# Loads, turns and layer steps at other distances in a fused attention and two-layer kernel

## The chip, the cores and the metric

The kernel runs on one core of a Trainium2 chip. The metric is the time of one execution on the device in microseconds (us); lower is better. A core has TensorE (PE, with its weight loads shown as PEld), VectorE (DVE), ScalarE (ACT), GpSimd (POOL) and SyncE (SP), each with its own queue of instructions that it works through in program order. DMAs are issued from the queues of SP and ACT.

## The reference

Inputs are q, k and v of shape 8 x 8 x 576 x 64 (batch, heads, rows, width), a threshold tau of 0.02, and the weights w_in (512 x 2048) and w_out (2048 x 512), all in 32 bits.

```python
scale = 1.0 / np.sqrt(q.shape[-1])
scores = scale * np.matmul(q, k.transpose(0, 1, 3, 2))
thresh = np.max(scores, axis=-1, keepdims=True) - tau
scores = np.where(scores >= thresh, scores, -1000000000.0)
scores = scores - np.max(scores, axis=-1, keepdims=True)
attn = np.exp(scores)
attn = attn / (np.sum(attn, axis=-1, keepdims=True) + 1e-09)
attn_out = np.matmul(attn, v)
x = attn_out.transpose(0, 2, 1, 3).reshape(B * S, H * D)   # 4608 x 512
h = x @ w_in
g = h - np.tanh(h)
out = g @ w_out
```

## The kernel before

**Pairs and tiles.** Two heads of one batch entry make a pair; there are 32 pairs, four to a batch entry. The 2 x 576 rows of q of a pair make nine tiles of 128 rows, 288 tiles in all. Eight of the nine lie in one head; the ninth holds the last 64 rows of both, and it is the last of an even pair and the first of an odd one. Even tiles are of kind A and odd ones of kind B; most work after the scores is done for an A and its B together.

**What is done to a pair.** q and k are loaded into `raw` tiles (L143 to L204). POOL scales them and splits each into two 16-bit halves, high and low (`split`, L222, three instructions). The split tile is turned so that the width lies on the partitions (`turn`, L297). Pairs 0 to 7 are turned on PE, nine transposes into a tile of PSUM from the pool `ps_big`, which DVE copies to SBUF (L313); pairs from `DUAL` = 8 on are turned by one transposing DMA each for k and q on SP's queue (L301). `swap` (L318) has POOL copy the turned k with its two halves exchanged (kS). `split_v` (L255) has POOL cast v into one of four tiles `vb`. The pools of `raw`, `hl` (split) and `qk` (kT, kS and qT) have two buffers for each name.

**What is done to a tile.** PE computes its scores from kT, kS and qT (L396, or L387 for the shared ninth tiles); DVE scales them into `sc` and keeps their maximum (L406) and makes the bias `nb` (L418); ACT makes `z` with a steep Prelu (L433), which leaves what lies within tau of the maximum and sends the rest far down; z is turned, on PE for pairs 0 to 5 and by a transposing DMA on SP (L440) from pair 6 on; ACT takes the exponential (L461 or L469) into `pT`; PE multiplies by v into `psO` (`attend`, L474); DVE divides (`norm`, L517); PE turns the result (`emit_x`, L537, `psX`) and DVE copies it into `xT`.

**The layers.** One stage m takes 512 rows of one batch entry (the last stage, the 64 remaining rows of all eight). An "h" step is a chunk of 128 of the 2048 hidden columns: four matmuls into `psH` (L565), tanh on ACT into `th` (L578), the subtraction on DVE into `g` (L584). A "y" step is a quarter of the second product for 128 rows: four matmuls into `psY` (L591), and after the fourth quarter a copy `yo` (L603) and a store. `psH` and `psX` share two buffers of PSUM; `psY` has one.

**Order.** The program is unrolled by hand into steps s from -8 to about 291 (the loop at L820). A step issues the scores of tile s + 8, z of tile s + 5, the tanh of h steps of the step before, the exponential of tile s, the layer step of this step if there is one, the subtraction of the h step before, and attend of tile s - 2. At its end it issues what `plan` has for this step: loads, splits, turns, swaps. A last part issues the loads and casts of the weights (POOL casts them at 16 listed steps, `cast_when`). For pair p the plan counts back from step 9p - 8, at which the pair's first tile gets its scores: an entry `("k0", 17)` of `LATER` loads k 17 steps earlier, "q0", "q1", "v0", "v1" are parts of loads, "ks", "qs", "vs" splits, "kt", "qt" turns, "kw" the swap. `LATER` holds for pairs from 8 on, one list for even and one for odd ones; `PREP` and `k_lead` hold for pairs 1 to 7. Loads of pairs from 8 on are issued from ACT's queue (L172), those before from SP's.

The layer steps of stage m = 0 to 6 run beside the attention of the next batch entry, from step 36 (m + 1) + 4 on. `PATTERN` (L622) gives for each of 36 steps whether it holds an h step, a y step or none. The first y steps of a stage are those left over from the stage before. The end, stages 7 and 8, is layers alone.

Of the kernel before, what the change touches and what calls it, by code (L numbers as in the profile page):

```python
# [9 lines left out]
F32 = mybir.dt.float32  # L10
# [8 lines left out]
def kernel(  # L19
# [11 lines left out]
    nc = tc.nc  # L31
    P = 128

    B, H, S, D = q.shape
# [11 lines left out]
    HPAIR = H // 2  # L46
# [5 lines left out]
    TPP = 9  # L52
# [10 lines left out]
    AHEAD = 8  # L63
# [25 lines left out]
    for i in range(NV):  # L89
        vb = const.tile([P, 2, 6, D + 1], BF16, name=f"vb{i}")  # L90
# [8 lines left out]
    for i in range(6):  # L99
# [8 lines left out]
    pool = lambda name, bufs, **kw: ctx.enter_context(  # L108
        tc.tile_pool(name=name, bufs=bufs, **kw)
    )  # L110
    PSUM = bass.MemoryType.PSUM
    raw_pool = pool("raw", 2)
    hl_pool = pool("hl", 2)
    qk_pool = pool("qk", 2)
    sc_pool = pool("sc", AHEAD - MASK + 2)
    st_pool = pool("st", 12)
    z_pool = pool("z", 4)
# [16 lines left out]
    raws = {}  # L134
    DUAL = 8
    AT_ONCE = 1
# [4 lines left out]
    boths = {}  # L141

    def load_part(p, t, part):  # L143


        b, h0 = p // HPAIR, 2 * (p % HPAIR)
        if part == 0:
            both = raw_pool.tile([P, 2, 10, D], F32, name=f"{t}raw", tag=t)
            both = boths[t] = both[:, 0:AT_ONCE, :, :]
            for a in range(AT_ONCE):  # L150
                raws[p + a, t] = both[:, a, :, :]
        both = boths[t]
        rows = {"k": k, "q": q, "v": v}[t][b, h0 : h0 + 2 * AT_ONCE, :, :]
        heads = both.rearrange("p a (h c) d -> p (a h) (c d)", h=2)
        if t == "k":
            dst = both[:, :, 0:TPP, :].rearrange("p a c d -> p a (c d)")
            rows = rows.rearrange("(a h) s d -> a (h s) d", h=2).rearrange(
                "a (p c) d -> p a (c d)", c=TPP
            )
        elif t == "v":  # L160
            rows = rows.rearrange("h (p c) d -> p h (c d)", c=TPP)
            if part == 0:
                dst, rows = heads[0:64, :, 0 : 4 * D], rows[:, :, 0 : 4 * D]
            else:
                dst, rows = heads[64:P, :, :], rows[:, :, 4 * D :]
        elif part == 0:
            dst = heads[:, :, 0 : 4 * D]
            rows = rows[:, 0:512, :].rearrange("h (p c) d -> p h (c d)", c=4)
        else:
            dst = both[:, part - 1, 4, :]  # L170
            rows = rows[2 * part - 2 : 2 * part, 512:S, :].rearrange("h s d -> s h d")
        LOADER.dma_start(out=dst, in_=rows)  # L172

    def load(p, t):
        b, h0 = p // HPAIR, 2 * (p % HPAIR)
        hs = slice(h0, h0 + 2)
        src = {"k": k, "q": q, "v": v}[t]
        eng = nc.sync
        r = raw_pool.tile([P, 2, 10, D], F32, name=f"{t}raw", tag=t)[:, 0, :, :]
        raws[p, t] = r  # L180
        eng.dma_start(
            out=r.rearrange("p (h c) d -> p h (c d)", h=2)[:, :, 0 : 4 * D],
            in_=src[b, hs, 0:512, :].rearrange("h (p c) d -> p h (c d)", c=4),
        )
        rem = src[b, hs, 512:S, :].rearrange("h s d -> s h d")
        if t == "v":
            eng.dma_start(out=r[0:64, 4:10:5, :], in_=rem)
        else:
            eng.dma_start(out=r[:, 4, :], in_=rem)

    def load_first(t, h, eng):

        src = {"k": k, "q": q}[t]
        if (0, t) not in raws:
            raws[0, t] = raw_pool.tile([P, 2, 10, D], F32, name=f"{t}raw", tag=t)[:, 0, :, :]
        r = raws[0, t]
        if h is None:
            rem = src[0, 0:2, 512:S, :].rearrange("h s d -> s h d")
            eng.dma_start(out=r[:, 4, :], in_=rem)
        else:  # L200
            eng.dma_start(
                out=r[:, 5 * h : 5 * h + 4, :].rearrange("p c d -> p (c d)"),
                in_=src[0, h, 0:512, :].rearrange("(p c) d -> p (c d)", c=4),
            )  # L204
# [49 lines left out]

    def split_v(p):  # L255
        r, vb = raws.pop((p, "v")), vbs[p % NV]
        lo = 64 if p >= DUAL else 0
        nc.gpsimd.tensor_copy(
            out=vb[:, :, 0:4, 0:D],
            in_=r.rearrange("p (h c) d -> p h c d", h=2)[:, :, 0:4, :],  # L260
        )
        nc.gpsimd.tensor_copy(out=vb[0:64, :, 4, 0:D], in_=r[lo : lo + 64, 4:10:5, :])
        nc.gpsimd.tensor_copy(out=vb[64:P, :, 5, 0:D], in_=r[lo : lo + 64, 4:10:5, :])

# [12 lines left out]
    def turn_chunk(out, c, lhsT, mixed=True):  # L277
# [4 lines left out]
            out=out, lhsT=lhsT, rhs=rhs, is_transpose=True, start=True, stop=True  # L282
        )

    def k_lead(p):
        if p < HPAIR + 2:
            return 6 if p in (2, 4) or p == HPAIR + 1 else 5 - (p == 1)
        return (6, 6)[1 - p % 2]

    def q_by_dma(p):  # L290

        return p >= DUAL

    def k_by_dma(p):
        return p >= DUAL

    def turn(p, t):  # L297
        hl = hls.pop((p, t))
# [290 lines left out]
    def project(m, ms, part, ps, last, cols=slice(0, d_model)):  # L589
# [31 lines left out]

    PATTERN = lambda m: {  # L622
        0: '-h--h-hh--h-hh-h-hh-h--hh-h--hh-y-yy',
        B - 2: 'hyhyhyhyhyhyhyhyhyhyhyhyhyhyhyhy',
    }.get(m, 'h-yhyhhyhyyhyyhh-yhhyhhy-yhyyh-yyhhy')

    FIRST = 3
    quarters = lambda m: [(m, ms, part) for ms in range(4) for part in range(4)]
# [90 lines left out]
    def w_load(piece):  # L719
# [6 lines left out]
        else:  # L726
# [18 lines left out]

    LATER = {
        0: (
            ("k0", 17), ("q0", 15), ("v0", 13), ("kt", 7), ("q1", 15),
            ("ks", 8), ("v1", 12), ("vs", 6), ("qs", 10), ("qt", 7),
            ("kw", 3),  # L750
        ),
        1: (
            ("k0", 19), ("v1", 14), ("q0", 18), ("v0", 16), ("qs", 11),
            ("q1", 17), ("qt", 8), ("ks", 13), ("vs", 6), ("kt", 10),
            ("kw", 7),
        ),
    }
    for p in range(DUAL, NPAIR):
        first = TPP * p - AHEAD
        at = lambda d, f: plan.setdefault(first - d, []).append(f)  # L760
        for what, d in LATER[p % 2]:
            t, w = what
            f = {
                "0": lambda p=p, t=t: load_part(p, t, 0),
                "1": lambda p=p, t=t: load_part(p, t, 1),
                "2": lambda p=p, t=t: load_part(p, t, 2),
                "s": lambda p=p, t=t: split_v(p) if t == "v" else split(p, t),
                "t": lambda p=p, t=t: turn(p, t),
                "w": lambda p=p, t=t: swap(p) if k_by_dma(p) else None,
            }[w]  # L770
            at(d, f)
    for p in range(1, DUAL):
        first = TPP * p - AHEAD
        for d, f in PREP[3 if p == 1 else 0 :]:
            d -= p == 1 and d == 3
            if p > HPAIR and d >= LDK - 2:
                d = ((16, 14, 12), (17, 15, 13))[1 - p % 2][LDK - d]
            elif d in (7, 8) and q_by_dma(p):
                d = ((9, 9) if d == 7 else (10, 10))[1 - p % 2]
            elif d == 4:  # L780
                d = 4
            elif d == 5:
                d = k_lead(p)
            elif p in (2, 4):
                d = {8: 9, 7: 8}.get(d, d)
            plan.setdefault(first - d, []).append(lambda p=p, f=f: f(p))
        d = (6, 7)[1 - p % 2] if q_by_dma(p) else 3 - (p == 1 or p >= 5)
        d = 4 if p in (2, 4) else d
        plan.setdefault(first - d, []).append(lambda p=p: turn(p, "q"))

    load(0, "v")
# [8 lines left out]
        load(1, t)  # L800
    pieces = w_pieces()
    load_when = [3, 8, 13, 18, 21, 25, 29, 34, 38, 42, 46, 49, 52, 55, 58, 61]
    cast_when = [11, 19, 27] + [4 * i + 32 for i in range(3)] + [3 * i + 44 for i in range(10)]

    todo, stage = [], 0
    fold = const.tile([P, 64], BF16, name="fold")
# [3 lines left out]
            plan.setdefault(-AHEAD, []).extend(plan.pop(at))  # L810


    kinks, wts, atts = {}, {}, {}
    for i in range(NTILE + 3):
        at = i - 4 if i < HPAIR * TPP else i
        atts.setdefault(at + LAG, []).append(i)
        if i < NTILE:
            wts.setdefault(at, []).append(i)
            kinks.setdefault(i // 2 * 2 + 2 - AHEAD if i < 4 else i - MASK, []).append(i)
    for s in range(-AHEAD, NTILE + LAG + 3):  # L820
        p, j = divmod(max(s, 0), TPP)
# [10 lines left out]
        n = s + AHEAD  # L832
# [14 lines left out]
        if s == 0:  # L847
            nc.vector.tensor_tensor(
                out=fold, in0=ident_bf[:, 0:64], in1=ident_bf[:, 64:P], op=ALU.add
# [15 lines left out]
                emit_x(pp - 1)  # L865
        for step in plan.pop(s, []):
            step()
        if s + AHEAD in cast_when:
            w_cast()
        if s + AHEAD in load_when:  # L870
            w_load(next(pieces))

    for _, step in todo:
# [16 lines left out]
    _ = bass_utils  # L890
# [35 lines left out]
```

## Time and profile before

| | us |
|---|---|
| median of 3 runs | 514.31 (512.71 to 514.61) |
| the profiled execution | 509.47 |
| its span, first to last instruction | 507.7 |

| engine | busy us | share of the span |
|---|---|---|
| PE | 484.1 | 95% |
| ACT | 432.7 | 85% |
| DVE | 400.0 | 79% |
| POOL | 291.1 | 57% |

The profile shows one execution, so its parts add up to 507.7 us and not to the median. A line of a group reads: line of the code, engine, operation, output<-inputs, shapes, count, then busy time and mean of one in ns, then the idle time of the engine ahead of it and what ended it. Overlapping matmuls are shown with their latency, so a busy PE may still be pausing; the distance from one start to the next tells more. A wait for several semaphores is put down to the one that came last.

### The profile page before, as it was taken

Reading aid. Unit: us, or ns where it says so; the run is one execution under the profiler, and the core shown is the slowest. Engines: PE = TensorE matmul, PEld = TensorE weight load, DVE = VectorE, ACT = ScalarE, POOL = GpSimd, SP = SyncE. Lnnn points to the kernel's source line nnn. Section 1 sums busy time; section 2 is a strip of 40 time slices with the busy share of each in tenths; the row PEclk is TensorE's granted clock in tenths of the full one; section 3 lists DMA queues with packets and bytes.
Section 4 is the critical chain, followed back from the end, with each engine's and each line's share of the span. In section 5 each row is a group of like instructions: output and inputs, shape, how many; then the busy total and the mean of one; then the engine's idle time right before and its main releaser. Section 6 shows DMA issues by size and latency. Waiting matters only on the chain.

```text
span 507.7 us, 12146 instructions
## 1 busy us (share of the span) xinstructions
PE 484.1 (95%) x4274; PEld 270.4 (53%) x4336; DVE 400.0 (79%) x1149; ACT 432.7 (85%) x617; POOL 291.1 (57%) x390
## 2 busy tenths in 40 slices
PE   8999899888999999999999999999998999999997
PEld 4667566444555555555555555555554555544444
DVE  5899979976989898988898889889887887544440
ACT  5999999988999999999999999999998999533430
POOL 7999999967676657574757575575567500000000
PEclk9999999998999999999999999999999999999999
DMA  6852658999999999999999999999999976211013
GB/s 198 264 163 90 196 176 220 226 189 220 211 245 228 242 227 223 242 249 211 228 228 268 216 228 228 223 231 231 212 220 252 197 131 113 76 41 43 24 40 83
DMA packets 234525, 95.61 MB, mean 188 GB/s; under 512 B 205152, under 2 KB 223840, under 8 KB 234464
## 3 DMA queue, kind: packets, MB, share of 16 engines
q1 hardware_dynamic: 213520, 73.17, 74.7%
q10 hardware_dynamic: 20944, 21.67, 15.7%
q8 instruction: 34, 0.56, 0.5%
q14 instruction: 27, 0.22, 0.1%
HBM read 36.70 MB, written 9.44 MB: 91 GB/s over the span
## 4 chain that ended last, share of the span: by engine, by line
PE 61%; POOL 12%; DMA 10%; ACT 6%; issue 5%; DVE 3%; ACTq 1%; SPq 0%; POOLq 0%
PE psY L591 20%; PE psH L565 16%; PE psS L396 14%; PE psO L499 4%; DMA zT<-z 3%; POOL kS L323 3%; PE psHt L565 3%; ACT pT L469 3%; ACT z L433 2%; DMA kT<-khl 2%; DMA kraw<-in_k_dram 2%; PE psS L387 2%; ACT th L578 1%; POOL w_in_sb L717 1%; DMA qraw<-in_q_dram 1%
## 5 line engine op out<-in xcount | busy, mean ns | idle before, releaser
L406 DVE TENSOR_SCALAR_CACHE_REDUCE sc<-psS 128x576 f32<-128x576 f32 x288 | 213.2, 752 | 28.7 <-PE psS L396 14.2
L433 ACT ACTIVATE z<-sc,nb 128x576 bf16<-128x576 f32 x288 | 217.2, 770 | 13.5 <-DVE nb L418 9.4
L591 PE MATMUL psY<-w_out_sb,g 128*128 128x512 bf16 (+1 forms) x564 | 141.5, 375 | 1.7 <-DVE nb L418 0.2
L469 ACT ACTIVATE pT<-zT 128x1152 f16<-128x1152 bf16 x117 | 135.0, 1154 | 4.6 <-DMA zT<-z 4.6
L565 PE MATMUL psH<-xT,w_in_sb 128*128 128x512 bf16 x448 | 118.8, 379 | 5.3 <-DVE g L584 2.2
L323 POOL COPY kS<-kT 64x1152 f16<-64x1152 f16 x62 | 70.7, 1141 | 74.6 <-DMA kT<-khl 55.2
L584 DVE SCALAR_TENSOR_TENSOR g<-th,psH 128x512 bf16<-128x512 f32 x128 | 87.6, 684 | 28.9 <-ACT th L578 28.1
L396 PE MATMUL psS<-kT,qT 128*128 128x512 f16 (+1 forms) x512 | 104.8, 286 | 3.3 <-DVE sc L406 1.5
L396 PE MATMUL psS<-kS,qT 128*128 128x512 f16 (+1 forms) x512 | 104.9, 287 | 0.1
L396 PEld LDWEIGHTS <-qT 128*128 128x128 f16 x1024 | 72.8, 98 | 58.6 <-issue 4.2
L578 ACT ACTIVATE th<-psH 128x512 f32<-128x512 f32 x128 | 74.6, 583 | 20.9 <-PE psH L565 20.9
L591 PEld LDWEIGHTS <-g 128*128 128x128 bf16 x592 | 51.3, 98 | 55.1 <-issue 1.1
L565 PEld LDWEIGHTS <-w_in_sb 128*128 128x128 bf16 x576 | 49.0, 98 | 57.3 <-issue 5.5
L499 PE MATMUL psO<-vb,pT 128*128 128x65 bf16 x1024 | 53.6, 195 | 0.0
L499 PEld LDWEIGHTS <-pT 128*128 128x128 f16 x1024 | 44.5, 98 | 9.9
L229 POOL TENSOR_TENSOR qhl<-qraw,qhl 128x576 f16<-128x576 f32 x31 | 39.7, 1281 | 2.6
L229 POOL TENSOR_TENSOR khl<-kraw,khl 128x576 f16<-128x576 f32 x31 | 39.7, 1280 | 2.6
L461 ACT ACTIVATE pT<-psZ 128x512 f16<-128x512 bf16 (+1 forms) x54 | 35.1, 653 | 2.5 <-PE psZ L452 2.3
L225 POOL TENSOR_SCALAR qraw<-qraw 128x576 f32<-128x576 f32 x31 | 20.8, 670 | 20.9 <-DMA qraw<-in_q_dram 19.6
L603 DVE COPY yo<-psY 128x512 f32<-128x512 f32 (+1 forms) x31 | 21.1, 680 | 13.3 <-PE psY L591 12.4
L492 PE MATMUL psO<-vb,pT 128*128 128x130 bf16 x128 | 28.3, 221 | 2.1 <-ACT pT L469 1.8
L525 DVE TENSOR_TENSOR osb<-psO,rc 128x256 bf16<-128x256 f32 x64 | 27.2, 425 | 2.2
(77 smaller groups left out, 448.6 us busy)
## 6 DMA issues: line engine op xcount, KB each, us to landing
out_dram<-yo SPq DMA_DIRECT2D x32, 256.0 KB, 2.9
kraw<-in_k_dram ACTq DMA_DIRECT2D x24, 288.0 KB, 4.2
qraw<-in_q_dram ACTq DMA_DIRECT2D x24, 256.0 KB, 4.1
wt<-in_moe_w_in_dram SPq DMA_DIRECT2D x8, 512.0 KB, 4.6
wt<-in_moe_w_out_dram SPq DMA_DIRECT2D x8, 512.0 KB, 4.2
vraw<-in_v_dram ACTq DMA_DIRECT2D x24, 160.0 KB, 4.0
vraw<-in_v_dram ACTq DMA_DIRECT2D x24, 128.0 KB, 4.2
vraw<-in_v_dram SPq DMA_DIRECT2D x8, 256.0 KB, 3.6
```

Of the source, the lines that this page charges most:

```text
L229: nc.gpsimd.tensor_tensor(out=hl[:, :, 1, :], in0=x, in1=hl[:, :, 0, :], op=ALU.subtract)
L323: nc.gpsimd.tensor_copy(out=o, in_=i)
L396: nc.tensor.matmul(out=ps[:, dst], lhsT=lhs, rhs=cols(p, kk, hh), start=(n == 0), stop=(n == 1),)
L406: nc.vector.tensor_scalar(out=sc, in0=ps[:, lo : lo + S], scalar1=SC, scalar2=None, op0=ALU.mult, op1=ALU.max, accum_out=mx[:, c : c + 1],)
L433: nc.scalar.activation(out=z, in_=sc, func=ACT.Prelu, bias=nb, scale=1.0, alpha=STEEP)
L461: nc.scalar.activation(out=pt[:, off * P : (off + n) * P], in_=ps[:, 0 : n * P], func=ACT.Exp)
L469: nc.scalar.activation(out=pt[:, 0 : n * P], in_=zts.pop(i)[:, 0:n, :], func=ACT.Exp)
L499: nc.tensor.matmul(out=po[:, t - 1 + ab, :], lhsT=pt[:, blk * P : (blk + 1) * P], rhs=vb[:, hh, c, :], start=False, stop=(n == 7), skip_gr ...
L565: nc.tensor.matmul(out=ps, lhsT=w_in_sb[:, c, n * P : (n + 1) * P], rhs=xs[m][:, c, :] if m < B else xR[:, c, :, :], start=(c == 0), stop= ...
L578: nc.scalar.activation(out=th, in_=ps, func=ACT.Tanh)
L584: nc.vector.scalar_tensor_tensor(out=gs[m][:, n, :], in0=th, scalar=-1.0, in1=ps, op0=ALU.mult, op1=ALU.add,)
L591: nc.tensor.matmul(out=ps, lhsT=gs[m][:, n, ms * P : (ms + 1) * P], rhs=w_out_sb[:, n, cols], start=(n == 0), stop=(n == DF_C - 1),)
```

## The change

- **v in one DMA.** For pairs from 8 on, `load_part` brings v of a pair with one DMA on 64 partitions (nine rows each) instead of two with 64 each, and `split_v` makes four copies of 64 partitions instead of one of 128 and two of 64. The entries "v1" go.
- **Buffers.** The `qk` pool gets three buffers for each of kT, kS and qT. The raw tiles of k and q become half as large, which they can since only half was used.
- **Pair 8's k on PE.** `k_by_dma` begins at pair 9; pair 8's k is turned like that of pairs 1 to 7, with its swap straight after. Its q is still turned by DMA.
- **Distances.** `LATER` has other distances and another order, and pairs 8 and 9 get lists of their own (`FIRST_LATER`). `LEADS` writes out the distances of pairs 1 to 7 for the splits and turns.
- **Layer steps.** The pattern of stages 2 to 5 is another, and stage 1 has its own.
- `SOONER` and the written-out list `cast_when` are other ways to put down values.

```diff
-    qk_pool = pool("qk", 2)
+    qk_pool = pool("qk", 3)
...
-            if part == 0:
-                dst, rows = heads[0:64, :, 0 : 4 * D], rows[:, :, 0 : 4 * D]
-            else:
-                dst, rows = heads[64:P, :, :], rows[:, :, 4 * D :]
+            dst = raws[p, t][0:64, :, 0:TPP, :].rearrange("p h c d -> p h (c d)")
...
     def split_v(p):
         r, vb = raws.pop((p, "v")), vbs[p % NV]
-        lo = 64 if p >= DUAL else 0
+        if p >= DUAL:
+            for at, c in ((0, 0), (64, 4)):
+                half = slice(at, at + 64)
+                nc.gpsimd.tensor_copy(out=vb[half, :, 0:4, 0:D], in_=r[0:64, :, c : c + 4, :])
+            for at in (0, 64):
+                nc.gpsimd.tensor_copy(
+                    out=vb[at : at + 64, :, 4 + at // 64, 0:D], in_=r[0:64, :, 8, :]
+                )
+            return
...
+    LEADS = {
+        1: (8, 7, 4, 4, 2),
+        2: (9, 8, 6, 4, 4),
+        3: (8, 7, 5, 4, 3),
+        4: (9, 8, 6, 4, 4),
+        5: (8, 7, 5, 4, 2),
+        6: (8, 7, 6, 4, 2),
+        7: (8, 7, 6, 4, 2),
+    }
...
     def k_by_dma(p):
-        return p >= DUAL
+        return p > DUAL
...
         0: '-h--h-hh--h-hh-h-hh-h--hh-h--hh-y-yy',
+        1: '-hhyhyyyh-yhhyy-hyyhyhh-hyyhyhyhyhyh',
         B - 2: 'hyhyhyhyhyhyhyhyhyhyhyhyhyhyhyhy',
-    }.get(m, 'h-yhyhhyhyyhyyhh-yhhyhhy-yhyyh-yyhhy')
+    }.get(m, 'hh-yhyyhhyyhyhy-y-hhhyyy-hhyyhyhhhyy')
...
     LATER = {
         0: (
-            ("k0", 17), ("q0", 15), ("v0", 13), ("kt", 7), ("q1", 15),
-            ("ks", 8), ("v1", 12), ("vs", 6), ("qs", 10), ("qt", 7),
-            ("kw", 3),
+            ("k0", 21), ("q0", 18), ("v0", 14), ("kt", 9), ("q1", 17),
+            ("ks", 10), ("vs", 6), ("qs", 8), ("qt", 7), ("kw", 5),
         ),
         1: (
-            ("k0", 19), ("v1", 14), ("q0", 18), ("v0", 16), ("qs", 11),
-            ("q1", 17), ("qt", 8), ("ks", 13), ("vs", 6), ("kt", 10),
-            ("kw", 7),
+            ("k0", 20), ("q0", 18), ("v0", 14), ("qs", 9), ("q1", 16),
+            ("qt", 7), ("ks", 14), ("vs", 3), ("kt", 10), ("kw", 2),
+        ),
+    }
+    FIRST_LATER = {
+        8: (
+            ("kw", -1), ("vs", 4), ("qt", 6), ("kt", 8), ("ks", 10),
+            ("k0", 19), ("v0", 14), ("q0", 21), ("qs", 8), ("q1", 21),
+        ),
+        9: (
+            ("q0", 19), ("qs", 11), ("q1", 18), ("vs", 5), ("k0", 21),
+            ("v0", 12), ("kw", 2), ("kt", 11), ("qt", 7), ("ks", 14),
         ),
     }
...
-        for what, d in LATER[p % 2]:
+        for what, d in FIRST_LATER.get(p) or LATER[p % 2]:
...
+            elif p in LEADS and d in (8, 7, 5, 4):
+                d = LEADS[p][(8, 7, 5, 4).index(d)]
...
-        d = 4 if p in (2, 4) else d
+        d = LEADS[p][4] if p in LEADS else d
...
+    SOONER = (4, 4, 4, 4, 0, 0, 0)
...
-        at = i - 4 if i < HPAIR * TPP else i
+        at = i - SOONER[min(i // TPP, 6)]
```

More of the change, by code (lines that the diff above doesn't have):

```diff
@@ L147, in load_part @@
         if part == 0:
[L148 to L151, printed above, removed]
+            n = 2 if t == "v" else 1
+            both = raw_pool.tile([P, n, 10, D], F32, name=f"{t}raw", tag=t)
+            boths[t] = both
+            raws[p, t] = both if t == "v" else both[:, 0, :, :]
         both = boths[t]
@@ L178, in load @@
         eng = nc.sync
-        r = raw_pool.tile([P, 2, 10, D], F32, name=f"{t}raw", tag=t)[:, 0, :, :]
+        n = 2 if t == "v" else 1
+        r = raw_pool.tile([P, n, 10, D], F32, name=f"{t}raw", tag=t)[:, 0, :, :]
         raws[p, t] = r
@@ L194, in load_first @@
         if (0, t) not in raws:
-            raws[0, t] = raw_pool.tile([P, 2, 10, D], F32, name=f"{t}raw", tag=t)[:, 0, :, :]
+            raws[0, t] = raw_pool.tile([P, AT_ONCE, 10, D], F32, name=f"{t}raw", tag=t)[:, 0, :, :]
         r = raws[0, t]
@@ L261, in split_v @@
         )
-        nc.gpsimd.tensor_copy(out=vb[0:64, :, 4, 0:D], in_=r[lo : lo + 64, 4:10:5, :])
-        nc.gpsimd.tensor_copy(out=vb[64:P, :, 5, 0:D], in_=r[lo : lo + 64, 4:10:5, :])
+        nc.gpsimd.tensor_copy(out=vb[0:64, :, 4, 0:D], in_=r[0:64, 4:10:5, :])
+        nc.gpsimd.tensor_copy(out=vb[64:P, :, 5, 0:D], in_=r[0:64, 4:10:5, :])
     mats = {}
@@ L802 @@
     load_when = [3, 8, 13, 18, 21, 25, 29, 34, 38, 42, 46, 49, 52, 55, 58, 61]
-    cast_when = [11, 19, 27] + [4 * i + 32 for i in range(3)] + [3 * i + 44 for i in range(10)]
+    cast_when = [11, 19, 27, 32, 36, 40, 44, 47, 50, 53, 56, 59, 62, 65, 68, 71]
     todo, stage = [], 0
@@ L867 @@
             step()
-        if s + AHEAD in cast_when:
+        for _ in range(cast_when.count(s + AHEAD)):
             w_cast()
-        if s + AHEAD in load_when:
+        for _ in range(load_when.count(s + AHEAD)):
             w_load(next(pieces))
```

## Prediction

> **What bounds the kernel now.** I read four views in turn: the page, busy time by stage, the waits of the stage that stands out, and one stretch of ACT's timeline. The page gives the tables of engines and slices:
>
> ```profile
> PE 484.1 (95%) x4274; PEld 270.4 (53%) x4336; DVE 400.0 (79%) x1149; ACT 432.7 (85%) x617; POOL 291.1 (57%) x390
> ...
> PE   8999899888999999999999999999998999999997
> POOL 7999999967676657574757575575567500000000
> ```
>
> A modelled busy time of PE hides pauses, so the stages come next (start:end, length, then busy time of PE, PEld, DVE, ACT and POOL, granted clock, DMA share, GB/s):
>
> ```profile
> 6.30:60.00 53.70, 48.66 (x653) 33.85 (x653) 48.05 (x147) 50.18 (x82) 50.49 (x65) 1.00 0.61 185
> 60.00:100.00 40.00, 37.40 (x408) 23.60 (x413) 34.63 (x101) 37.29 (x59) 37.18 (x48) 1.00 0.82 202
> 100.00:125.00 25.00, 20.36 (x181) 11.20 (x182) 17.57 (x55) 21.67 (x31) 17.79 (x23) 0.93 1.21 201
> 125.00:325.00 200.00, 197.63 (x1743) 108.66 (x1773) 177.78 (x523) 194.82 (x265) 129.31 (x163) 1.00 1.17 231
> 325.00:440.00 115.00, 111.16 (x970) 60.65 (x986) 93.73 (x273) 104.00 (x142) 52.41 (x68) 1.00 1.02 194
> 440.00:507.70 67.70, 63.87 (x310) 30.24 (x311) 26.10 (x40) 22.40 (x38) 0.00 (x0) 0.99 0.15 44
> ```
>
> To 100 us ACT and POOL are 93 to 94% busy and PE waits for them. From 125 to 325 us PE never rests: the first reductions L406 of successive pairs stand 14.27, 13.04, 12.54, 13.04 us apart, and this group of four repeats to 0.01 us. Nothing is to be won there except from less PE work. The weak stage is 100 to 125 us, where pairs 8 to 10 change over to turning by DMA. A second place is after 325 us: pair 25 takes 14.11 us instead of 13.04 and pair 29 takes 15.55, together 3.6 us late. The end, from 440 us, is PE alone.
>
> The waits from 60 to 125 us (who, for whom: total us, times, longest) and ACT's own timeline:
>
> ```profile
> DVE g L584 <- ACT th L578: 4.2, 5, 1.5
> ...
> PE psO L492 <- ACT pT L469: 1.8, 1, 1.8
> ...
> ACT z L433 <- DVE sc L406: 1.6, 1, 1.6
> ```
> ```profile
> 112.87 0.58 ACT L578 ACTIVATE th<-psH 128x512 f32<-128x512 f32 x1
> 114.37 0.60 ACTq L172 DMA_DIRECT2D vraw<-in_v_dram  x1
> 115.02 0.78 ACT L433 ACTIVATE z<-sc,nb 128x576 bf16<-128x576 f32 x1 [1.57 <-DVE sc L406]
> ```
>
> ACT stops for 1.57 us. The releaser named is DVE, but what held it is the line between: ACT's queue was to issue the second v load of pair 10 and did so at 114.37. In the trace all DMAs share eight completion semaphores, taken in turn. This load's semaphore was last used by the turn of q of pair 9, issued at 106.37 and landed at 114.35. So an ACT load waits until the DMA about eight places back has landed, and everything behind it on ACT waits too. PE then stood 1.98 us for pT (115.39 to 117.37), and from 117.4 to 120.8 us the granted clock was 0.50: another 1.7 us lost.
>
> [...] Here the half clock lasted 3.4 us, after a pause of only 1.98 us with thin work before it. [...] here their starts are 55 ns apart, and I use that. [...] the 128x512 copy at L258 takes 617 ns, and I use this for 64x512.
>
> **The change, part by part.**
>
> Same values: SOONER and the list of cast steps come out as before. LEADS moves only the k turn of pair 5, from step 31 to 32: nothing. So the first 43 steps (70 us) stay.
>
> *v in one DMA* removes 24 issues at L172, 0.6 us each on ACT's queue (mostly beside a running activation), and 24 of the page's 393 places in the semaphore rotation. Counting places in program order, 57 of 120 ACT loads had five steps to the DMA eight places back; now 13 of 96 have five, and 78 have six or seven. A step is 1.47 us and a turn lands in 3.4 to 8.0 us, so five steps (7.3 us) can block and seven (10.3) do not. The splits of v become 2x617 + 2x292 ns = 1.82 us instead of 1.20. That is 0.62 us more POOL per pair, hidden in steady state, where POOL is 65% busy and waits 36.7 us for kT; it isn't hidden for pairs 8 and 9, where POOL is full.
>
> *Pair 8 turns k on PE.* Added: 9 transposes x 0.055 = 0.5 us PE, one copy of 0.76 us on DVE. Removed: a transposing DMA that occupied SP's queue from 93.22 to 95.81 and kept both qT and zT waiting behind it (ACT then waited 0.89 us for that zT, PE 1.08 us for g). PE waits for ACT in this stage, so its 0.5 us costs nothing if q is there. But swap (2.33 us) now comes ahead of q's split on POOL. POOL is full until 86.4 us; then ks8 2.8, a cast 1.0 (90.2), a pause for kT8 until step 56's copy (about 92.6), swap to 95.0, q's split to about 97.7. q was split at 89.16 before. The turn of q goes out near 97.8 instead of 95.91 and lands after 3.4 to 8.0, median 4.9: about 102.7, for scores that PE could start at 100. Before, it landed at 101.35 and PE waited 0.79. So PE waits about 2.5 us here. What hides most of it is that ACT reads these scores only three steps later (sc72 at 102.4, z72 at 107.6). I charge 0.9.
>
> The changeover sums to: ACT's blocks at 80.6, 93.7, 102.3 and 115.0 (0.46 + 0.41 + 0.89 + 1.57) less that 0.9 and about 0.1 for POOL, plus 1.7 of half clock = 4.0 us gained. Bounds: a late q with a clock drop makes it 2 us lost; all PE pauses from 60 to 125 us that are not ACT's work would make it 7 gained.
>
> *Three buffers and longer distances, later pairs.* Even pairs' kT and swap come 2 steps earlier, their k and q loads 2 to 4 steps; the ten loads per two pairs, which lay within 12 of 18 steps, are now eight spread over 16. Odd pairs' swap is put 5 steps later, 2 before its scores, and their v load 2 later; but POOL works in program order as its inputs come, waits 36.7 us for kT in the repeating part, and so does this swap as soon as kT lands. PE waits for none of these there: zero. What they can mend are the 3.6 us of pairs 25 and 29: pT waited 0.45, 0.88 and 2.03 us for zT that took 6 to 7 us to land beside a burst of loads. I take 2.8; bounds 0 and 3.6.
>
> *Layer steps.* PE's step is 1.35 us (even) or 1.66 (odd, with attend). psH has two buffers, so the third h of "hhh" needs the g of the first about 2.1 us after its psH; "hh" needed it never. From psH's end to g's end the trace of m=2 to 4 shows 2.0 to 3.2 us. Laid over the rows from 202.42 us (psH), 203.87 (th), 204.75 to 205.43 (g), the third h wants to start at 205.44 and gets its buffer just then: about 0.15 us each, twice in each of m=2 to 5, 8 x 0.15 = 1.2. Two y either side of a row block are now neighbours once per stage and the yo copy (0.68) stands between: 4 x 0.1 = 0.4. Stage m=1 ends in h and m=2 starts "hh": with psX between, the h needs the previous step's g, 1.3 us once. Together 2.9 lost; bounds 0 (their own queues absorb it) and 8 x 0.8 + 4 x 0.7 + 1.9 = 11.1 at the slow end of the 2.0 to 3.2.
>
> **Sum**: -4.0 - 2.8 + 2.9 = -3.9 us. The profiled execution took 509.47 us (span 507.7), so its like would take 505.6; the median shown, 514.31, is 4.8 us above it, and the same difference gives 510.4.
>
> **Rivals.**
> *Layers go smoothly.* With g at 2.0 us after psH the third h does not wait: -4.0 - 3.6 + 0 = -7.6, 506.7. For it: 2.00 to 2.13 us at five of 16 places. Against: 2.7 to 3.2 at six.
> *q of pair 8 eats the gain.* Its turn takes the 8.0 us seen at 106.37, 3.1 more than the median, and a pause that long brings the half clock's 1.7 back: -4.0 + 4.8 - 2.8 + 2.9 = +0.9, 515.2: no change. For it: POOL's order. Against: ACT's three steps of stock.
> *Slower: the psH buffer.* The third h of each triple waits 0.8 us, the neighbours 0.7, the seam of m=1 and 2 1.9: 11.1 lost in the stage where PE has no slack, against 6.8 gained: +4.3, 518.6. It decides from 0.5 us per triple (8 x 0.5 with the others at 2.8 outweigh 6.8). For it: ACT is 97% busy there and three z and th in a row exceed PE's steps (1.83 against 1.5 us). Against: three y follow at once.
>
> **Numbers.** Forecast 0.42, smooth layers 0.20, q of pair 8 0.18, psH buffer 0.20. A measurement here can tell about 0.5% (2.6 us) from no change. Faster 0.62, same 0.18, slower 0.20. The likeliest time is 510.4; faster cases alone reach from 503 to 511.7. The range is 503 to 518, leaving out the far part of the slow case and very little below.
>
> **What would show it.** Right: no v wait on ACT and no 0.50 clock near 117 us; PE's pause near step 64 (about 100 us) for qT of 1 to 3 us; pairs 25 and 29 at the length of their like; L565 waiting for g at offsets 20 and 33 of m=2 to 5 by some 0.1 us. Wrong: a PE pause at 100 us above 4 us, a repeating group longer than 53.5 us, or a stage before 70 us that moved.

## The result and the profile after

The changed kernel is slower: 518.96 us (median of 5 runs, 514.03 to 520.98) against 514.31 for the kernel before on the same chip; ratio 1.0123 [1.0076, 1.0170]. The forecast was 510.4, range 503 to 518. A ratio here compares the runs near each kernel's fastest, while a median is of all runs, so the two can differ, in one run below by 0.9 per cent. The profiled execution took 520.98 us, span 519.2.

The page of the changed kernel, its tables of engines and slices, and two rows of its table of DMA issues (engine, kind, count, KB each, us from issue to landing):

```profile
PE 492.0 (95%) x4345; PEld 271.9 (52%) x4345; DVE 399.6 (77%) x1150; ACT 432.5 (83%) x617; POOL 304.9 (59%) x414
...
PE   8999899799999999999989999999988999999997
POOL 8999998796758574866777666767536700000000
...
vraw<-in_v_dram ACTq DMA_DIRECT2D x24, 288.0 KB, 4.9
...
zT<-z SPq DMA_TRANSPOSE x117, 4.8
```

The amount of work is as before, but for POOL's copies of v: 304.9 us busy against 291.1. (PE's busy time counts the latency of late matmuls too, and the profile of before lacks the records of some 60 of them.) What moved is the landing of DMAs: in the profile of before, v's two halves of 160 and 128 KB had 4.0 and 4.2 us, and zT 4.4.

Busy time by stage, columns as before:

```profile
100.00:125.00 25.00, 22.01 (x196) 12.01 (x195) 19.54 (x64) 22.73 (x31) 19.89 (x28) 0.93 1.16 209
125.00:325.00 200.00, 194.28 (x1709) 104.83 (x1708) 168.70 (x499) 186.50 (x255) 136.29 (x176) 1.00 1.19 225
325.00:440.00 115.00, 109.34 (x951) 58.81 (x950) 93.75 (x276) 104.73 (x144) 59.82 (x79) 1.00 1.08 192
```

From 125 to 325 us ACT did 255 instructions instead of 265 and DVE 499 instead of 523: this stage, where the forecast saw nothing to win and a loss from the layer steps alone, ran late. From 100 to 125 us the granted clock is 0.93, as before.

The first reductions of the pairs (`sc`, L406 before, L424 after) tell the same by place:

| first reduction of pair | before, us | after, us | after minus before |
|---|---|---|---|
| 7 | 89.7 | 90.2 | +0.5 |
| 8 | 102.4 | 105.3 | +2.9 |
| 9 | 117.7 | 118.5 | +0.8 |
| 10 | 131.5 | 131.2 | -0.3 |
| 12 | 158.8 | 158.4 | -0.4 |
| 31 | 413.9 | 425.4 | +11.5 |

So two things failed. The changeover of pairs 8 to 10, where 4.0 us were to be won, won nothing. And 11.9 us went between pairs 12 and 31. The end after the last score is the same (81.0 and 81.1 us). These are two single executions, and they overstate the difference: the profile of before lies 4.8 us under its median, that of the changed kernel 2.0 us over its own.

**The changeover.** PE's timeline of the changed kernel, and the window after it (columns of the stages):

```profile
101.57 0.42 PE L517 MATMUL psO<-vb,pT 128*128 128x65 bf16 x8
104.52 0.42 PE L414 MATMUL psS<-kT,qT 128*128 128x512 f16 x2 [2.53 <-DMA qT<-qhl]
...
105.02 1.62 PE L583 MATMUL psH<-xT,w_in_sb 128*128 128x512 bf16 x4
106.44 0.69 PE L414 MATMUL psS<-kT,qT 128*128 128x512 f16 x2
```
```profile
105.30:108.70 3.40, 3.40 (x16) 1.64 (x15) 2.42 (x6) 1.52 (x3) 3.25 (x5) 0.50 1.63 242
```

PE stands 2.53 us for pair 8's qT, the pause that the forecast put at 2.5. Then a half clock: four matmuls into psH take 1.62 us instead of 1.02, and for 3.4 us the granted clock is 0.50. And ACT, whose stock of three steps was to hide most of it, ran dry:

```profile
106.74 0.60 ACT L596 ACTIVATE th<-psH 128x512 f32<-128x512 f32 x1 [1.44 <-PE psH L583]
107.78 1.16 ACT L487 ACTIVATE pT<-zT 128x1152 f16<-128x1152 bf16 x1 [0.44 <-DMA zT<-z]
```

ACT takes its queue in order here: tile 71's z, whose scores and bias DVE had done at 102.39 us, starts at 108.85, behind this tanh and this exponential. The tanh needs the matmuls into psH, and these stand behind the late scores on PE and then run at half clock. A stock of scores doesn't cover that.

**The later stage.** Two answers on one tile, zT: the kernel before, then the changed one (issue on SP's queue, min/median/max ns; then what ACT waited for, us and times):

```profile
L440 SPq DMA_TRANSPOSE zT<-z x117: 1242/1411/2533, 81.4 to 431.4; - x117
...
  DMA zT<-z: 4.6, 5
```
```profile
L458 SPq DMA_TRANSPOSE zT<-z x117: 1242/1513/5152, 81.0 to 442.9; - x117
...
  DMA zT<-z: 16.9, 15
```

ACT's exponential waits 16.9 us for turned z instead of 4.6. From 125 to 410 us the mean from a zT's issue to its landing is 5.14 us against 4.60 before, and what is left between landing and use is 1.41 us against 1.99. SP's queue shows how one late turn holds the next; here around pair 28, which took 17.55 us instead of 12.54:

```profile
380.82 2.54 SPq L319 DMA_TRANSPOSE kT<-khl  x1
383.45 4.63 SPq L458 DMA_TRANSPOSE zT<-z  x2
388.18 1.54 SPq L319 DMA_TRANSPOSE qT<-qhl  x1
389.82 3.48 SPq L458 DMA_TRANSPOSE zT<-z  x1
```

From 380.8 to 393.3 us SP issues turns almost without a gap. Over the whole profile an issue of zT takes SP 1.80 us on average, against 1.54 before, and the next zT starts late as well (0.94 us from z's end to the issue of its turn on average, 0.55 before).

### The profile page after: what moved, and what is told of

Read it like the earlier page. It is cut to its first block, busy times and chain, and to the rows that moved or that the text cites. A ratio compares the mean times of both kernels' runs of the same rounds, so it can differ in the third digit from the quotient of the medians.

```text
span 519.2 us, 12216 instructions
## 1 busy us (share of the span) xinstructions
PE 492.0 (95%) x4345; PEld 271.9 (52%) x4345; DVE 399.6 (77%) x1150; ACT 432.5 (83%) x617; POOL 304.9 (59%) x414
## 4 chain that ended last, share of the span: by engine, by line
POOL 42%; PE 25%; issue 19%; ACT 6%; DMA 6%; DVE 2%; ACTq 0%; SPq 0%; POOLq 0%; DVEq 0%
POOL kS L341 10%; PE psY L609 10%; PE psH L583 6%; POOL qhl L227 6%; POOL khl L227 5%; POOL vb L259 4%; DMA zT<-z 4%; POOL kraw L223 3%; POOL khl L226 3%; POOL qraw L223 3%; POOL qhl L226 3%; PE psS L414 3%; PE psHt L583 3%; POOL vb L261 2%; ACT z L451 2%
## 5 line engine op out<-in xcount | busy, mean ns | idle before, releaser
L424 DVE TENSOR_SCALAR_CACHE_REDUCE sc<-psS 128x576 f32<-128x576 f32 x288 | 213.4, 752 | 28.2 <-PE psS L414 20.7
L487 ACT ACTIVATE pT<-zT 128x1152 f16<-128x1152 bf16 x117 | 135.1, 1155 | 17.0 <-DMA zT<-z 16.9
L609 PE MATMUL psY<-w_out_sb,g 128*128 128x512 bf16 (+1 forms) x592 | 145.7, 373 | 0.8 <-DVE yo L621 0.6
L583 PE MATMUL psH<-xT,w_in_sb 128*128 128x512 bf16 x480 | 123.9, 380 | 5.4 <-DVE g L602 5.1
L259 POOL CAST vb<-vraw 64x512 bf16<-64x512 f32 x48 | 29.5, 614 | 1.8 <-DMA vraw<-in_v_dram 0.7
```

What stands on the lines that cost most here:

```text
L259: nc.gpsimd.tensor_copy(out=vb[half, :, 0:4, 0:D], in_=r[0:64, :, c : c + 4, :])
L424: nc.vector.tensor_scalar(out=sc, in0=ps[:, lo : lo + S], scalar1=SC, scalar2=None, op0=ALU.mult, op1=ALU.max, accum_out=mx[:, c : c + 1],)
L487: nc.scalar.activation(out=pt[:, 0 : n * P], in_=zts.pop(i)[:, 0:n, :], func=ACT.Exp)
L583: nc.tensor.matmul(out=ps, lhsT=w_in_sb[:, c, n * P : (n + 1) * P], rhs=xs[m][:, c, :] if m < B else xR[:, c, :, :], start=(c == 0), stop= ...
L609: nc.tensor.matmul(out=ps, lhsT=gs[m][:, n, ms * P : (ms + 1) * P], rhs=w_out_sb[:, n, cols], start=(n == 0), stop=(n == DF_C - 1),)
```

## The experiments

The theories to be told apart: A, v in one DMA on 64 partitions slows the transfers around it; B, the longer POOL work of `split_v` delays turns and swaps; C, the layer patterns; D, the distances. For the changeover: the late split of pair 8's q. "zT" below is the mean from issue to landing from 125 to 410 us. It comes from the one profiled execution of each run, while the times are of all its executions.

**First, parts undone and parts alone.**

The changed kernel with the layer patterns of before:

```diff
-        1: '-hhyhyyyh-yhhyy-hyyhyhh-hyyhyhyhyhyh',
-    }.get(m, 'hh-yhyyhhyyhyhy-y-hhhyyy-hhyyhyhhhyy')
+    }.get(m, 'h-yhyhhyhyyhyyhh-yhhyhhy-yhyyh-yyhhy')
```

> The changed kernel with the layer patterns of before (no pattern of its own for stage 1). Theory L (the new layer steps make PE wait for g and the psH buffer): 513 to 515 us, 4 to 6 below the changed kernel. Theory D (the new distances make zT late on SP's queue): 518 to 520, no change from the changed kernel; ACT still waits some 15 us in all for zT.

520.41 us, 1.0020 [0.9865, 1.0174]. Its runs lay between 508 and 526; this tells nothing.

The kernel before with the new patterns (the same lines the other way round):

> The kernel before with nothing changed but the layer patterns. Theory L: 517 to 520 us, with PE waits for g (L565) at the triples of h. Theory D: 513 to 516, and ACT's wait for zT stays near 5 us.

513.61 us, 0.9995 [0.9967, 1.0024]. No cost of the patterns is seen there; the interval leaves room for 1.2 us.

The kernel before with v in one DMA and the four copies:

```diff
-                dst, rows = heads[0:64, :, 0 : 4 * D], rows[:, :, 0 : 4 * D]
+            dst = raws[p, t][0:64, :, 0:TPP, :].rearrange("p h c d -> p h (c d)")
...
-            ("ks", 8), ("v1", 12), ("vs", 6), ("qs", 10), ("qt", 7),
+            ("ks", 8), ("vs", 6), ("qs", 10), ("qt", 7),
```

> The kernel before with v of pairs from 8 on in one DMA on 64 partitions and the four-copy split, all else as before. Theory V (the one DMA of 288 KB slows the transposing DMAs beside it): 517 to 520 us, zT landing 0.4 us or more later on average. Theories L and D: 512 to 514, since the block of ACT near 115 us goes and nothing else changes.

517.09 us, 1.0084 [1.0049, 1.0118]; zT 5.15. This part alone makes the kernel before slower (by the medians 1.6 us, by the ratio 4.3).

The changed kernel with v in two DMAs as before:

> The changed kernel with v in two DMAs and the three-copy split as before; the second part one step after the first. Theory V: 513 to 515 us. Theories L and D: 518 to 521, with more DMAs on ACT's queue waiting for a semaphore.

516.25 us, 1.0026 [0.9986, 1.0067]; zT 4.93. By the ratio most of the loss is gone.

**Then: its DMA or its copies?** The kernel before with its 128x512 copy of v made twice, so that POOL has the added work (306.3 us busy in all, 305.6 in the run with one DMA and four copies), and the loads stay:

```diff
-        nc.gpsimd.tensor_copy(
+        for _ in range(2 if p >= DUAL else 1):
+            nc.gpsimd.tensor_copy(
```

> The kernel before with the 128x512 cast of v done twice for pairs from 8 on (0.62 us more of POOL per pair, as the four copies cost), and v still in two DMAs. If POOL's extra work is what makes v in one DMA slow: 517 to 520 us, ratio about 1.008. If the DMA is: 514 to 516, ratio within 0.3% of 1.

515.38 us, 0.9978 [0.9945, 1.0010]. POOL's work is not the cause: B falls. But this run's profiled execution was a late one, 518.92 us, and in it zT lands in 5.09 us, with v in two DMAs. The row of its page for the exponential:

```profile
L470 ACT ACTIVATE pT<-zT 128x1152 f16<-128x1152 bf16 x117 | 135.2, 1156 | 18.6 <-DMA zT<-z 18.3
```

So a late zT is seen in a late execution of either kind. The zT of one profile doesn't tell the loads of v apart; the times of many executions must, and the landing of v itself.

The kernel before with the one DMA, but one of the two 64x512 copies left out:

```diff
-            for at, c in ((0, 0), (64, 4)):
+            for at, c in ((0, 0),):
```

> The kernel before with v in one DMA on 64 partitions and one of the two 64x512 copies left out for pairs from 8 on, so that POOL's work is 1.2 us per pair as before (half of v's main keys stay stale). If POOL's extra work is the cause: 513 to 515 us, ratio 0.995 to 1. If the DMA is: 516 to 519, ratio about 1.008, zT landing 0.4 us later than before.

517.73 us, 1.0046 [1.0016, 1.0076]; zT 5.08. POOL's work is back at that of the kernel before (289.8 us busy against 291.1), and the loss stays: it is the DMA. Nor is it the time that ACT's queue gives to the loads of v, one issue of 0.64 us for a pair here against two of 0.61 before.

The kernel before with v in one DMA on 128 partitions, as k is loaded:

```diff
+            dst = both[:, :, 0:TPP, :].rearrange("p a c d -> p a (c d)")
+            rows = rows.rearrange("(a h) s d -> a (h s) d", h=2).rearrange(
+                "a (p c) d -> p a (c d)", c=TPP
+            )
```

> The kernel before with v of a pair in one DMA on all 128 partitions, one piece of 2304 bytes each, as k is loaded; three copies as before (v's rows lie in another order than the weights, so the product is another). If it is the 64 partitions, two pieces each, that slow the DMAs: 513 to 515 us. If it is the larger pieces or one DMA of 288 KB as such: 516 to 519, ratio about 1.008.

509.14 us (six executions), 0.9880 [0.9835, 0.9926]; zT 4.60. In this and the run ahead of it the DMA has the same number of bytes, in pieces of the same size (2304 B, 128 of them). What differs in the load is 64 or 128 partitions, and the order in which DRAM is read. Their rows for v on ACT's queue with the landing times, and ACT's waits for zT, 64 partitions first:

```profile
L168 ACTq DMA_DIRECT2D vraw<-in_v_dram x24: 631/641/663, 83.1 to 397.5; - x24
...
DMA to landing us min/median/max: 2.6/4.9/6.9
```
```profile
L171 ACTq DMA_DIRECT2D vraw<-in_v_dram x24: 329/339/393, 83.1 to 388.1; - x24
...
DMA to landing us min/median/max: 2.6/3.7/6.4
```
```profile
ACT pT L475 <- DMA zT<-z: 19.9, 23, 3.0
```
```profile
ACT pT L468 <- DMA zT<-z: 13.2, 10, 2.4
```

(The landing rows take in the early loads on SP's queue too; of the 24 on ACT's alone the means from 125 us on are 5.32 and 4.05 us.)

64 partitions with each partition's two pieces side by side in DRAM, to see whether the order of reading matters:

```diff
+            rows = rows.rearrange("h (p a c) d -> (h p) a (c d)", a=2, c=TPP)
```

> The kernel before with one v DMA on 64 partitions whose two pieces per partition are neighbours in DRAM (v's rows lie in another order, and one of the two 64x512 copies is left out). If it is where the bytes land (two pieces on each of 64 partitions): ratio 1.004 to 1.009, 516 to 519 us. If it is the order of the reads in DRAM: ratio about 0.988, 508 to 511.

516.51 us (six executions), 1.0122 [1.0042, 1.0202]; v lands in 5.26 us. It doesn't: where the data goes decides, not the order in which it is read.

**The distances and buffers.** The changed kernel with v in two DMAs and the old patterns, so that distances, buffers and pair 8 are what is left of the change:

> The changed kernel with v in two DMAs (second part a step after the first), three copies, and the layer patterns of before: what is left is the new distances, the third buffers and pair 8's k on PE. If v in one DMA is the whole loss: within 0.4% of before, 514 to 517 us. If the new distances cost by themselves: 518 or more, ratio 1.006 or more.

512.82 us, 0.9973 [0.9946, 1.0000]. At most a small gain, with q of pair 8 still late (PE pauses 1.29 us for it).

**v on 128 partitions in the whole kernel.** A partition then holds rows of one head, and the split becomes eight small copies:

```diff
+            for h in range(2):
+                own_h = slice(64 * h, 64 * h + 64)
+                for at, c in ((0, 0), (64, 4)):
+                    half = slice(at, at + 64)
+                    nc.gpsimd.tensor_copy(out=vb[half, h, 0:4, 0:D], in_=r[own_h, c : c + 4, :])
+                    nc.gpsimd.tensor_copy(out=vb[half, h, 4 + at // 64, 0:D], in_=r[own_h, 8, :])
```

In the changed kernel:

> The changed kernel with v in one DMA on all 128 partitions (as k is loaded) and a split of eight small copies on POOL that shift halves by 64 partitions, so that the product is the same. If the 64-partition landing is the loss: 507 to 511 us, ratio 0.985 to 0.995, zT landing in about 4.7 us. If the new distances lose with any single v DMA: 515 or more.

514.37 us, 1.0032 [0.9992, 1.0071]; zT 4.89. This missed the 507 to 511 us expected: q of pair 8 is late here too, and PE pauses 3.12 us for it with a half clock after. In the kernel before:

> The kernel before with v in one DMA on all 128 partitions and the eight-copy split, its own distances and layers. If the DMA's form is what counts and POOL's extra 0.8 us or so per pair is hidden: 508 to 511 us, ratio about 0.988 as in the run without the copies' shift. If POOL's longer split holds up kT: 513 or more.

510.71 us against 515.42 for the kernel before on the same chip, ratio 1.0002 [0.9961, 1.0043]; zT 4.64. The medians show a gain of 4.7 us and the ratio none; the ratio of 0.988 that was expected did not come. The changed kernel itself, beside them:

> The changed kernel once more, to size the loss beside the others on the same chip: ratio 1.008 to 1.016 by every theory; ACT waits 10 us or more for zT, and PE 2 to 3 us for qT of pair 8 near 102 us.

518.56 us (six executions), 1.0134 [1.0059, 1.0208]: the result again. In the changed kernel landing on 128 partitions is worth 4.2 us of the medians.

**Pair 8's q.** One edit to the changed kernel: q is split one step sooner, ahead of k's turn and swap, and turned one step sooner.

```diff
-            ("kw", -1), ("vs", 4), ("qt", 6), ("kt", 8), ("ks", 10),
-            ("k0", 19), ("v0", 14), ("q0", 21), ("qs", 8), ("q1", 21),
+            ("kw", -1), ("vs", 4), ("qs", 9), ("qt", 7), ("kt", 8), ("ks", 10),
+            ("k0", 19), ("v0", 14), ("q0", 21), ("q1", 21),
```

> The changed kernel with one edit: q of pair 8 is split one step earlier and ahead of k's turn and swap, so that its turning DMA goes out sooner. Theory A: PE's pause of 2.70 us at 101.8 us and the 0.50 clock from 105.3 us go, pair 9's first reduction comes at about 116 us instead of 118.5, and the time falls from about 519 to 516 to 518, ratio to before about 1.006 to 1.009. Theory B (the late q is hidden): pair 9 starts within 0.5 us of 118.5 and the ratio stays at 1.012. In both the later pairs stay slow, since v still lands on 64 partitions: zT lands in a mean of about 5.1 us.

515.70 us, 1.0041 [1.0007, 1.0075]. PE's timeline and the window of the half clock in this run:

```profile
103.78 0.39 PE L528 MATMUL psO<-vb,pT 128*128 128x130 bf16 x4
104.01 0.41 PE L414 MATMUL psS<-kT,qT 128*128 128x512 f16 x2
...
105.46 1.02 PE L583 MATMUL psH<-xT,w_in_sb 128*128 128x512 bf16 x4 [0.80 <-DVE g L602]
```
```profile
105.30:108.70 3.40, 2.65 (x30) 1.63 (x30) 3.37 (x11) 3.29 (x6) 3.20 (x6) 1.00 0.81 173
```

q's turn goes out at 93.8 us instead of 99.0, the pause and the half clock are gone, ACT is busy 3.29 of the 3.4 us instead of 1.52. Pair 9 starts at 116.2 us instead of 118.5 and pair 10 at 128.9 (before 131.5): here is the gain of the changeover.

How long PE pauses for a late q differs between executions: 1.28 to 3.19 us in the seven profiles with the late split. The half clock follows in four of them. In the changed kernel with the old patterns it does not:

```profile
104.33 0.42 PE L414 MATMUL psS<-kT,qT 128*128 128x512 f16 x2 [2.33 <-DMA qT<-qhl]
104.59 0.41 PE L414 MATMUL psS<-kS,qT 128*128 128x512 f16 x2
104.83 1.03 PE L583 MATMUL psH<-xT,w_in_sb 128*128 128x512 bf16 x4
```

v on 128 partitions with the old patterns, without and with this edit:

> The changed kernel with v of a pair in one DMA on 128 partitions (copied by eight small POOL copies) and with the layer patterns of the kernel before; all the rest as changed. Theory A (the landing on 64 partitions cost the time, the layer patterns some 2 us, the new distances and buffers are a small gain): zT lands in a mean of about 4.6 to 4.9 us from 125 to 410 us, the repeating group of four pairs is back at 52.9 us from about 53.4, and the time is about 2 us under the changed kernel with v on 128 partitions and its own patterns (514.4): 508 to 512, ratio to before about 0.993. Theory B (the patterns cost nothing, as in the kernel before): 513 to 515, ratio 1.00. Theory C (the new distances cost too): above 515, ratio over 1.004.

> The run with v on 128 partitions and the old layer patterns, and in addition q of pair 8 is split on POOL one step earlier and ahead of k's turn and swap. Theory A (the late split of q of pair 8 costs PE's pause near 101.8 us, 2.7 us, and the half clock after it, 1.7): the pause and the 0.50 clock go, pair 9's first reduction comes 1 to 3 us sooner, and the time is 1 to 3 us under the run without this edit. Theory B (the stock of three steps hides it, or k's late turn takes its place): the pause moves to k's turn and the time is within 1 us of the run without.

515.77 us, 1.0026 [0.9985, 1.0067], and 510.98 us, 0.9953 [0.9922, 0.9984]. The second of them is called the twin below. The edit is worth 4.8 us of the medians, more than the 1 to 3 expected; at the start of pair 10 the two profiles are 2.6 us apart, so part of it comes later, and from what isn't shown. The mean granted clock over all runs is 0.9951 without it and 0.9992 with it. The first missed what theory A expected: it said 508 to 512, for it did not count q of pair 8.

**All corners together on one chip.** With pair 8's q first: v on 128 partitions with the new patterns, v on 64 with the old ones, and v on 128 with the old ones again (the twin).

> The changed kernel, layer patterns included, with two edits: v of a pair in one DMA on 128 partitions, and q of pair 8 split first. Against the run that had these two and the old layer patterns (510.98, ratio 0.9953) only the patterns differ. Theory A (the new patterns cost 0.5 us per stage, 2 us in all, as the repeating group of 53.4 against 52.9 us suggests): 512 to 514, ratio about 0.999. Theory B (the new patterns have no net cost, as in the kernel before, where their looser places absorb late zT): within 1 us of its twin, ratio 0.993 to 0.997. Theory C (patterns cost more than 2 us here): above 514.

> The changed kernel with v of a pair in one DMA on 64 partitions as changed, the old layer patterns, and q of pair 8 split first. Against the twin with v on 128 partitions (510.98, ratio 0.9953) only the landing of v differs. Theory A (the landing on 64 partitions slows the transfers beside it): zT lands in a mean of 5.0 us or more against 4.83, and the time is 2 to 5 us above the twin: 513 to 516, ratio 1.000 to 1.008. Theory B (with q of pair 8 in time, nothing more is lost by v): within 1 us of the twin, ratio 0.993 to 0.997.

> The twin of the two others again, on the same chip as they: v on 128 partitions, the old layer patterns, q of pair 8 first. It gave 0.9953 [0.9922, 0.9984]. If it beats the kernel before, it does so again, 0.990 to 0.998, about 511 us; if that was the chip's luck, the ratio is 1.000 or more.

| with q of pair 8 first | median us | ratio |
|---|---|---|
| v on 128, new patterns | 510.86 | 0.9968 [0.9931, 1.0005] |
| v on 128, old patterns | 511.39 | 0.9985 [0.9953, 1.0017] |
| v on 64, old patterns | 515.47 | 1.0017 [0.9981, 1.0054] |
| the kernel before | 514.27 | 1 |

The patterns make no difference that can be seen: means over all runs 0.5 us apart, with a 95% interval of 2.0 either way. The landing makes one of 3.7 us (2.3 either way), 4.1 of the medians, and 1.6 to 2.5 by the ratios. The twin was shown faster once (0.9953) and not the second time, though its median is again 2.9 us under that of before: a version at about 511 us, by the medians some 3 us below the kernel before.

## Why the prediction was wrong

**What failed.** Two terms of the sum.

*v in one DMA* was priced as a gain alone: fewer issues, fewer semaphore places, hidden POOL copies. The term that was missing is the landing on 64 partitions. In eight profiles with it v lands in 5.05 to 5.48 us on average (from 125 us on); on 128 partitions, in seven, in 3.93 to 4.26; the halves of before, in five, in 4.00 to 4.42. zT follows less sharply: 4.96 to 5.38 us with 64, 4.60 to 4.91 with 128, and 4.60 to 5.11 with the halves. It does so in a stage where it had 2 us to spare on average and nothing in its worst places, and SP's queue was held longer by its turns. Measured in the changed kernel: 4.1 to 4.2 us of the medians between 64 and 128 partitions. That the time goes this way, through zT and SP's queue, is read from these waits; no run separates it.

For the same bytes the landing takes 1.27 us longer on 64 partitions (5.32 us against 4.05, beside other transfers). That partitions decide is shown; why they do is not, and no run here separates a reason. The kernel before had its halves of v on 64 partitions each as well, but one half on partitions 0 to 63 and the other on 64 to 127 (`heads[0:64]` and `heads[64:P]` in the diff); the one DMA puts all of v on the first 64. Whether it matters which 64 was not tested. One DMA on 128 was no slower for zT than the halves (4.60 and 4.64 us against 4.60).

*q of pair 8* was found, timed (2.5 us forecast, 2.53 measured; its turn out at 97.8 forecast, 99.0 measured) and charged 0.9. It cost more: 4.8 us of the medians with v on 128 partitions; in the changed kernel the edit brings the median from 518.56 to 515.70, 2.9 us, though on another chip; at the start of pair 10 the profiles show 2.3 to 2.6. The cover named, three steps of scores in stock, covers z but not the tanh of the layer step that stands behind the late scores on PE; and in four of seven profiles the half clock came back with the pause, which the sum left out and only the rival and the lower bound carried. That rival, "q of pair 8 eats the gain", had the mechanism in part, with 4.8 us: the half clock came, but the turn took 5.44 us and not 8.0, and it went out late because k's copy, for which the swap ahead of it waits, came at 93.8 us instead of 92.6. Its price for the rest was too good, since it too missed v.

**What held.** To 70 us nothing moved (0.5 us in the first reduction of pair 0, 0.2 us in those of pairs 1 to 6). With q in time the changeover gives what the step said in kind: no load holds ACT near 115 us, no half clock near 117, and pair 10 starts 2.6 us (q first in the changed kernel) to 3.4 us (the twin, the second time: 128.1) sooner than before in four of five profiles, against 4.0 forecast; in the fifth, with v on 64 partitions and the old patterns, 0.6. Not all of it lasts: pair 10 itself takes 13.73 to 16.47 us in these five instead of 14.27, and pair 11 starts 1.1 to 3.4 us sooner than before. The forecast has no such term, and why it is so stays open.

Most of the signs named for "right" came true in the changed kernel, though the time was wrong: PE's pause for qT, no v wait, no half clock near 117 us, pair 25 at the length of its like. So did one sign for "wrong": the groups of four pairs from pair 10 to 29 take 54.4 to 60.0 us.

*Later pairs, -2.8.* This came true where it was said. With the old distances and patterns pair 25 takes 13.96 to 15.07 us and pair 29 14.69 to 15.87 in all seven profiles. With the new distances pair 25 takes 12.78 to 13.04 in all twelve, and pair 29 13.64 to 13.96 in eleven of them. Between the profile of before and the twin's second one the two pairs make 2.7 us (14.11 + 15.55 against 13.04 + 13.90). That it is the distances is not shown, for in the kernel before with the new patterns alone they take 12.78 and 13.64. And the term counted two pairs only: others slipped in the changed kernel, pair 28 by 5 us.

*Layers, +2.9.* Measured between -2.5 and +1.4 in the time. In the run with both faults mended and new patterns PE's waits for g ahead of psH from 125 to 410 us are two (1.7 us), with the old ones three (2.4):

```profile
PE psH L581 <- DVE g L600: 1.7, 2, 1.6
```
```profile
PE psH L581 <- DVE g L600: 2.4, 3, 0.9
```

This refutes the psH rival, which has a wait of 0.8 us in each triple. It can't decide on the 0.15 us of the forecast, since such a view lists no wait under 0.15. An undisturbed group of four pairs is longer with the new patterns, 14.45 + 12.67 + 13.49 + 12.85 = 53.46 against 52.89 us. Over four stages that would be 2.3 us, not far from the term; why that doesn't show in the time is not settled. A looser pattern that absorbs late zT would do it, but that is only argued.

The psH rival gave 518.6 and so the right time, for a cause that the runs refute. With both faults mended and all else of the change in place the kernel takes 510.86 us, 3.4 less than before, and the forecast was -3.9. That the two are so near is luck: the +2.9 for the layers isn't seen in the time, the later slips were not in the sum, and part of the 3.4 may come from v on 128 partitions, which is no part of the change: alone it brought the median of the kernel before down by 4.7 and 5.4 us (by the ratio by nothing in one run and 1.2 per cent in the other). The two faults, 4.1 and 2.9 to 4.8, then lead back to 518 to 520.

**Still open.** With v in two DMAs the changed kernel came out at 1.0026 with the new patterns and 0.9973 with the old ones, on different chips; a difference of 2.7 us that the last table doesn't show. Why the twin's ratio went from 0.9953 to 0.9985 is open too, and so is what the change without its two faults is worth with v in its halves.

## What to carry to other kernels

Price a merged load by where it lands and by what lands beside it, not by the issues it saves. Here the turns beside it had 2 us to spare on average and nothing in the worst places, and the merged load, put on 64 partitions, took about 4 us more of the kernel than on 128. When a pause of PE is said to be hidden by a stock, go through everything queued behind it in program order, on PE and on the engine with the stock, and add the half clock that may follow (3.4 us at 0.50 in the changed kernel). A late pair in one profile is a gain to be had if other profiles show it late in the same place, as they did here; but count what slips elsewhere too, and judge by many executions.

## What was not expected of the hardware

- A DMA of 288 KB on 64 partitions holds ACT's queue 0.641 us at its issue and lands in 5.32 us on average; the same bytes in the same pieces on 128 partitions 0.339 and 4.05 us. Transposing DMAs beside it land in 5.08 and 4.60 us.
- The issue of a transposing DMA takes SP between 1.24 and 5.15 us (zT, changed kernel; up to 2.53 in the kernel before), and the next turn in SP's queue goes out only after it: near pair 28 five turns in a row fill SP from 380.8 to 393.3 us.
- A pause of PE of 2.53 us was followed by 3.4 us at half clock (granted clock 0.93 from 100 to 125 us), one of 3.19 us in the run with v on 128 partitions, the old patterns and the late q by 0.93 as well; one of 2.33 us by none. In all five profiles with q first that stage has 1.00.
- In the profiles of the kernel before and of the changed one the half clocks of 117.4 and of 105.3 us begin 112.640 and 98.987 us after the record of the first full clock, which is 33 and 29 times 3.4133 us, and each lasts 3.413 us. What makes one pause bring it and another not was not tested.
- POOL's copy of 64x512 takes 614 ns on average against 617 for 128x512 (changed kernel): the 617 ns that the prediction put in for 64x512, an estimate from the copy of 128x512, holds here.
